# Routing three finished row tiles with one set of VectorE instructions, and a different split of work in the last steps of an attention kernel

## The chip, the cores and the metric

The kernel runs on one core of one Trainium2 chip. The metric is the device time of one execution in microseconds (us); the median of three runs stands for it. TensorE (PE) does the matrix products, VectorE (DVE) and ScalarE (ACT) the elementwise work and the reductions, GpSimd (POOL) some elementwise work and the indirect DMAs, SyncE (SP) issues the other DMAs. Each engine works through its own instructions in their order and waits on semaphores for the others.

## What is computed

Three layers, one behind the other, in float32. First attention over q, k, v of shape (4, 8, 576, 64), in which each row keeps only its 32 largest scores. The result is turned into 2304 rows (tokens) of 512 numbers. Then two mixture-of-experts layers with 8 experts: each row goes to the expert with the largest gate logit. Cut to what matters:

```python
scores = scale * np.matmul(q, k.transpose(0, 1, 3, 2))
kth = np.partition(scores, -32, axis=-1)[..., -32:-31]
scores = np.where(scores >= kth, scores, -1e9)
attn = softmax(scores)                       # exp(x - max) / (sum + 1e-9)
x = np.matmul(attn, v)  ->  rows (2304, 512)
logits = x @ w_gate                          # 8 logits of a row
expert_idx = np.argmax(logits, axis=1)
gate_w = softmax(logits) at expert_idx
out[rows of e] = gate_w * (relu(xe @ w1[e]) @ w2[e])
# second layer: the same on the rows with x @ w_skip > 0, added to x
```

## The kernel before

Attention is cut into 72 groups g = 9 u + j. The unit u is one pair of batches with one pair of heads (8 units: two batch pairs times four head pairs), and j is one of nine row tiles of 128 rows. A group has two halves hh, one for each head, each with a score tile of 128x576.

A loop over steps tau writes out the program. In one step, different stages of different groups stand one behind the other, in an order that the list in `attention` gives: a stage of group g is placed at g plus a fixed distance, and the last six groups have small corrections (`TAIL`). The stages that this document speaks of, with the step of group g in which they stand:

- A1 (g+1): the search for the largest scores on VectorE (14 MAX8 of 82 or 83 columns, then smaller ones). T (g+1): `tm` on POOL.
- Bs (g+4): the signs `sg` on ScalarE, then the products `y` on POOL, two of each. C (g+5): the MAX8 on VectorE that reads `y`.
- Dr, Dm, Dz (g+8): the mask. It is made in one of three ways, by half. "Unmasked first": ScalarE has taken the exponential in the step before (Dx), and VectorE multiplies it by the comparison (`scalar_tensor_tensor`, line 287). Masked first by VectorE (`YS`): a `tensor_scalar` on VectorE (line 266), a subtraction on POOL (line 270), the exponential on ScalarE (line 278). Masked first by ScalarE (`XS`): a Relu on ScalarE (line 269) in place of the `tensor_scalar`. Over six groups, nine of the twelve halves are masked first; in the last `NX` groups none is.
- E (g+9): TensorE turns the probabilities (line 306), and two copies bring them from PSUM to `pT` (ScalarE, line 312; in the last `ND[hh]` groups VectorE, line 310).
- F (g+10): the product with v. FinP, Fin (g+11): the result is turned back, and VectorE writes it, scaled, into the row tile `x` and the shares of the gate logits into `parts` (line 340).
- Ga (g+12), Gr (g+14), for the groups of the units 3 and 7 only, in which a row tile becomes finished: the routing of the row tile. Ga puts seven small VectorE instructions (sum of the shares, maximum, first maximum as a one-hot `gob`) into the list `small`. Gr has an exponential on ScalarE, the ranks on TensorE and then the rest (place in the expert's region, 1/sum, the place as an integer `gix`), again through `small`, at last the indirect DMA (`scatter`, line 576) that writes the 128 rows to their places.

What is in `small` is issued by A1, one instruction behind each of its MAX8s; from step 74 on, with no A1 left, the whole list is issued at the end of each step.

Unit 3 is finished in the middle of attention, unit 7 at its end. The small tiles lg, order and places of a row lie in spare columns of the PSUM tile `s` of the scores. `one_port` (line 70) is a `tensor_scalar` in the form that also writes its accumulator. When all row tiles are scattered, the first expert layer loads its rows.

## Time and profile before

| | |
|---|---|
| median of three runs | 1063.95 us (1061.88 to 1067.97) |
| the profiled execution: time, span | 1056.39 us, 1054.6 us |
| mean granted TensorE clock | 0.954 of full speed |
| busy share of the span | PE 84%, DVE 72%, ACT 64%, POOL 60% |
| attention | from 0 to about 506 us |
| expert layers | from about 508 us to the end |

The shares are means over two parts with different limits. Attention has 20 slices of the 40 of the page: there VectorE is at 90% or more in slice after slice, while in the expert layers TensorE is.

### The profile page before, as it was taken

To read this page: it belongs to the slowest core of one execution; us is meant where nothing else is said; L and a number is where in the kernel's file an instruction comes from. 1 tells how busy PE (TensorE), PEld (TensorE's weight loads), DVE (VectorE), ACT (ScalarE), POOL (GpSimd) and SP (SyncE) were. 2 spreads that over 40 slices of the span, in tenths; PEclk is the share of its full clock that TensorE was granted. 3 is DMA by queue.
4 is the path that set the end of the run, shared out by engine and by line. 5 is a ranking of instruction groups with operands and counts; after the bars stand their busy time and mean duration, and the time that the engine had idled before them with its cause. 6 is when DMAs were issued, how large, how long until landed. Compare 5 with 4: busy or idle time off the path is not lost. (4 is left out here: it accounts for less than half of the span.)

```text
span 1054.6 us, 20835 instructions
## 1 busy us (share of the span) xinstructions
PE 884.0 (84%) x6315; PEld 699.0 (66%) x6315; DVE 759.8 (72%) x3581; ACT 674.5 (64%) x1362; POOL 628.4 (60%) x451
## 2 busy tenths in 40 slices
PE   7477878786777768887699999998998799999994
PEld 5355555554455545555588879877886788899883
DVE  7999999999999999999427545456563356644461
ACT  5599999988898989973335534554553454443340
POOL 2788887887888888863224344344533566564561
PEclk9699999989998999979799999999999899999997
DMA  9992010100302000001635544466633466665520
GB/s 307 320 278 68 2 46 24 46 24 21 109 32 89 22 21 21 2 1 52 225 120 183 171 144 152 140 200 182 188 112 108 149 222 208 217 201 178 167 86 14
DMA packets 55049, 127.88 MB, mean 121 GB/s; under 512 B 8105, under 2 KB 8105, under 8 KB 54864
## 3 DMA queue, kind: packets, MB, share of 16 engines
q1 hardware_dynamic: 48464, 112.89, 34.0%
q0 software_dynamic: 6400, 12.65, 3.2%
q8 instruction: 100, 1.64, 0.6%
q14 instruction: 85, 0.70, 0.2%
HBM read 96.04 MB, written 37.86 MB: 127 GB/s over the span
## 5 line engine op out<-in xcount | busy, mean ns | idle before, releaser
L692 POOL TENSOR_TENSOR w<-raw,w 128x1024 fp32r<-128x1024 f32 x74 | 179.4, 2436 | 192.0 <-ACT w L690 136.8
L224 POOL TENSOR_TENSOR y<-s,sg 128x576 f32<-128x576 f32 x144 | 208.4, 1468 | 52.8 <-ACT sg L221 43.3
L767 PE MATMUL y<-w,h 128*128 128x512 f32 x936 | 228.1, 396 | 8.3 <-DVEq L716 2.2
L743 PE MATMUL hp<-xT,w 128*128 128x192 f32 (+4 forms) x1536 | 213.6, 296 | 5.6 <-DVE h L758 3.0
L743 PEld LDWEIGHTS hp<-xT,w 128*128 128x128 f32 x1536 | 203.7, 190 | 9.8 <-DVE h L758 5.3
L767 PEld LDWEIGHTS y<-w,h 128*128 128x128 f32 x936 | 171.4, 188 | 50.1 <-issue 10.5
L193 DVE MAX8 ca<-s 128x8 f32<-128x82 f32 (+1 forms) x1008 | 160.1, 228 | 5.3 <-ACT s L182 5.3
L270 POOL TENSOR_TENSOR r<-s,r 128x576 f32<-128x576 f32 x96 | 135.7, 1427 | 17.8 <-DVE r L266 15.9
L690 ACT ACTIVATE w<-raw 128x1024 fp32r<-128x1024 f32 x128 | 133.5, 1054 | 0.5 <-ACTq L716 0.5
L758 DVE SCALAR_TENSOR_TENSOR h<-hp,h 128x512 fp32r<-128x512 f32 (+1 forms) x128 | 77.8, 619 | 76.5 <-ACT h L757 76.5
L757 ACT ACTIVATE h<-hp 128x512 fp32r<-128x512 f32 (+1 forms) x128 | 69.8, 545 | 97.0 <-PE hp L743 89.6
L306 PE MATMUL m<-ident,p 128*128 128x128 f32 x576 | 97.7, 297 | 37.9 <-DVE parts L340 19.2
L306 PEld LDWEIGHTS m<-ident,p 128*128 128x128 f32 x576 | 65.3, 147 | 79.9 <-ACT p L278 25.0
L221 ACT ACTIVATE sg<-s,tm 128x576 f32<-128x576 f32 x144 | 112.1, 800 | 8.4 <-POOL tm L212 8.4
L692 DVE TENSOR_TENSOR w<-raw,w 128x1024 fp32r<-128x1024 f32 x54 | 96.0, 1777 | 21.5 <-ACTq L716 12.8
L97 PE MATMUL s<-kT,qT 64*128 64x288 f32 x512 | 83.3, 444 | 24.2 <-ACT gex L596 14.6
L231 DVE MAX8 my<-y 128x8 f32<-128x576 f32 x144 | 101.6, 745 | 0.7 <-POOL y L224 0.6
L182 ACT ACTIVATE s<-s 128x1152 f32<-128x1152 f32 (+1 forms) x73 | 81.8, 1122 | 22.1 <-PE s L97 18.2
L134 PE MATMUL m<-pT,v 128*64 128x128 f32 (+1 forms) x1280 | 88.3, 285 | 7.2 <-ACT pT L312 5.4
L134 PEld LDWEIGHTS m<-pT,v 128*64 128x64 f32 x1280 | 69.8, 148 | 20.3 <-ACT pT L312 9.4
L312 ACT ACTIVATE pT<-m 128x512 f32<-128x512 f32 x137 | 76.9, 612 | 6.8 <-PE m L306 6.8
L278 ACT ACTIVATE p<-r,neg 128x576 f32<-128x576 f32 x96 | 75.4, 790 | 8.2 <-POOL r L270 7.9
(136 smaller groups left out, 1254.4 us busy)
## 6 DMA issues: line engine op xcount, KB each, us to landing
raw<-in_moe_w_dram SPq DMA_DIRECT2D x128, 512.0 KB, 4.4
x<-zrow SPq DMA_DIRECT2D x16, 1028.0 KB, 17.9
xg<-x SPq DMA_DIRECT2D x56, 257.0 KB, 3.7
v<-in_v_dram SPq DMA_DIRECT2D x8, 576.0 KB, 3.8
kT<-in_k_dram SPq DMA_DIRECT2D x7, 576.0 KB, 4.3
qT<-in_q_dram SPq DMA_DIRECT2D x7, 576.0 KB, 5.7
out_dram<-yo,ix POOLq DMA_INDIRECT x40, 4.9
kT<-in_k_dram SPq DMA_DIRECT2D x2, 288.0 KB, 3.5
```

Source lines behind the costliest of these rows:

```text
L97: nc.tensor.matmul(p[:, c, :288], d["qT"][h, b, t * 128:t * 128 + 128], d["kT"][h, b, cs], start=True, stop=True)
L134: nc.tensor.matmul(po[i * 64:i * 64 + 64, cs], d["vt"][:, b, i, c] if c < 4 else d["v8"][i * 64:i * 64 + 64, b], pts[i][:, c, cs] if c < 4 ...
L193: nc.vector.max(out=ca[:, c], in_=e["s"][hh][:, cut[c]:cut[c + 1]])
L221: nc.scalar.activation(sg, e["s"][hh], AF.Sign, bias=bt["tm"][:, w:w + 1], scale=-ONE_BELOW, accum_out=bt["ac"][:, w:w + 1])
L224: nc.gpsimd.tensor_mul(y, e["s"][hh], sg)
L231: nc.vector.max(out=bt["my"][:, 2 * i + hh, 8:], in_=e["y"][hh])
L270: nc.gpsimd.tensor_tensor(r, e["s"][hh], r, op=OP.subtract)
L306: nc.tensor.transpose(pp[:, c], e["p"][:, hh, c * 128:c * 128 + 128], ident)
L690: nc.scalar.activation(t[:, 0], raw, AF.Copy)
L692: eng.tensor_tensor(t[:, 1], raw, t[:, 0].bitcast(F32), op=OP.subtract)
L743: nc.tensor.matmul(p[:, :W], self.w1(g, c)[:, a, fs], x[:, c, b, :W], start=(i == 0), stop=(i == 11))
L767: nc.tensor.matmul(p, self.HT[f][:, a, js], self.W2[f // 2][:, b, f % 2 * 512:f % 2 * 512 + 512], start=(f + a + b == 0), stop=(f == 7 and ...
```

## The change

Three row tiles that lie side by side (j = 0 to 2, 3 to 5, 6 to 8) share one tile `x` and one tile `parts`, and are routed together when the third is finished; the very last one (j = 8 of the last unit) is routed alone, and the two before it as a pair. The instructions of the routing work on 128x3x8 elements, with `tensor_tensor` and `tensor_reduce` in place of the forms that take one scalar per row. Besides, `NX` goes from 8 to 3 (the groups 64 to 68 keep the mixed masks), and `ND` from (0, 7) to (0, 0) (ScalarE makes all copies to `pT`).

```diff
-NX = 8
-ND = (0, 7)
+NX = 3
+ND = (0, 0)
...
-            x[bp, j] = ev.xp.tile([128, HP * 128 + 2], F32, name="x", bufs=11)
+            x[bp, j // 3] = ev.xp.tile([128, 3, HP * 128 + 2], F32, name="x", bufs=4)
...
+        n = {NG - 2: 2, NG - 1: 1}.get(g, 3 if j % 3 == 2 else 0)
+        return (bp, j // 3, j % 3 + 1 - n, n) if hp == HP - 1 and n else None
...
+def gate_tiles(tc, ev, sb, x, parts, rt, places):
...
+    def rest():
+        nc.scalar.activation(ed, ed, AF.Exp)
+        nc.gpsimd.tensor_copy(x[:, :, Dm + 1], ev.tok[:, rt:rt + n])
+        p = ev.ps.tile([128, 4, 8], F32, name="m", bufs=ev.mb)
+        nc.tensor.matmul(p[:, :n + 1], ev.tri, ob[:, :n + 1], start=True, stop=False)
+        for k in range(n, 0, -1):
+            nc.tensor.matmul(p[:, n + 1 - k:n + 1], ev.ones, ob[:, :k], start=False, stop=(k == 1))
...
+    def empty():
+        nc.gpsimd.memset(ob[:, n], 0.0)
+        v.tensor_reduce(out=lg, in_=parts.rearrange("p t h e -> p t e h"), op=OP.add, axis=AX.X)
...
+    return [empty,
+            lambda: v.tensor_reduce(out=f[:, :, 0], in_=lg, op=OP.max, axis=AX.X),
+            lambda: v.tensor_tensor(order, lg, wide(f[:, :, 0:1]), op=OP.is_ge),
+            lambda: v.tensor_tensor(ed, lg, wide(f[:, :, 0:1]), op=OP.subtract),
+            lambda: v.tensor_tensor(order, order, ev.rev8[:, None, :].to_broadcast([128, n, 8]), op=OP.mult),
+            lambda: v.tensor_reduce(out=f[:, :, 1], in_=order, op=OP.max, axis=AX.X),
+            lambda: v.tensor_tensor(ob[:, :n], order, wide(f[:, :, 1:2]), op=OP.is_equal)], rest, [
+            lambda: v.tensor_tensor(row, at[0][:, :n], base[:, None, :].to_broadcast([128, n, 8]), op=OP.add),
+            lambda: v.tensor_tensor(base, at[0][:, n], base, op=OP.add),
+            lambda: v.tensor_tensor(mine, row, ob[:, :n], op=OP.mult),
+            lambda: v.tensor_reduce(out=f[:, :, 3], in_=ed, op=OP.add, axis=AX.X),
+            lambda: v.tensor_reduce(out=f[:, :, 2], in_=mine, op=OP.add, axis=AX.X),
+            lambda: v.tensor_scalar(f[:, :, 3], f[:, :, 3], 1e-9, None, op0=OP.add),
+            lambda: v.tensor_copy(ix[:, :n], f[:, :, 2]),
+            lambda: v.reciprocal(x[:, :, Dm], f[:, :, 3])] + [
+            lambda t=t: scatter(tc, ev, ev.rows[0], ix[:, t:t + 1], x[:, t], ev.group) for t in range(n)]
```

In the changed program two of these carry line numbers that are named later: the `tensor_scalar` that adds 1e-9 is line 642 and the cast to `tix` line 643; both read and write SBUF.

VectorE, middle of attention (unit 3). Before, the second half of one row tile's routing stands between the MAX8s of A1; `gf`, `gob` and `gix` are its small tiles:

```order
L564 TENSOR_TENSOR s<-m,base_90 128x8
L565 TENSOR_TENSOR base_90<-m,base_90 128x8
L193 MAX ca<-s 128x8
L601 TENSOR_SCALAR gf<-gf 128x1
L193 MAX ca<-s 128x8
L568 SCALAR_TENSOR_TENSOR gf<-s,gob 128x8
L193 MAX ca<-s 128x8
L602 RECIPROCAL x<-gf 128x1
L193 MAX ca<-s 128x8
L603 CAST gix<-gf 128x1
```

In the changed program the second half for three row tiles, with `tf`, `ted`, `tob` and `tix` in their place, ends like this:

```order
L639 TENSOR_TENSOR s<-s,tob 128x24
L193 MAX ca<-s 128x8
L640 TENSOR_REDUCE tf<-ted 128x3
L193 MAX ca<-s 128x8
L641 TENSOR_REDUCE tf<-s 128x3
L193 MAX ca<-s 128x8
L642 TENSOR_SCALAR tf<-tf 128x3
L193 MAX ca<-s 128x8
L643 CAST tix<-tf 128x3
L193 MAX ca<-s 128x8
L644 RECIPROCAL x<-tf 128x3
```

One such set stands in every third step in place of one in each, and the addition and the cast work on three elements of a partition instead of one.

POOL, from the last `tm` (step 72) to the end of attention. Before, the products `y` of the groups 69 to 71 stand alone, and then come nine copies and nine scatters in turn:

```order
L212 TENSOR_SCALAR tm<-my 128x6
L224 TENSOR_TENSOR y<-s,sg 128x576 x6
L597 COPY x<-tok 128x1
L576 DMA x_82<-x,gix 18432x514
L597 COPY x<-tok 128x1
L576 DMA x_82<-x,gix 18432x514
```

In the changed program the subtractions `r` of the groups 65 to 68 stand between them, and the scatters come three, three, two and one at a time:

```order
L212 TENSOR_SCALAR tm<-my 128x6
L270 TENSOR_TENSOR r<-s,r 128x576 x2
L224 TENSOR_TENSOR y<-s,sg 128x576 x2
L270 TENSOR_TENSOR r<-s,r 128x576 x2
L224 TENSOR_TENSOR y<-s,sg 128x576 x2
L270 TENSOR_TENSOR r<-s,r 128x576 x2
L224 TENSOR_TENSOR y<-s,sg 128x576 x2
L270 TENSOR_TENSOR r<-s,r 128x576
L627 MEMSET tob 128x8
L619 COPY x<-tok 128x3
L573 DMA x_82<-x,tix 18432x514 x3
```

Seven more POOL instructions of 576 columns stand behind the last `tm` than before, and an eighth in front of it.

## Rows read from the trace of the kernel before

**Rows 1.** Busy time by stretch: stretch, length, engines (count), TensorE clock, DMA share, GB/s

```profile
250.00:300.00 50.00, 34.91 (x321) 23.25 (x320) 49.55 (x332) 42.99 (x106) 40.61 (x39) 0.97 0.22 74
460.00:480.00 20.00, 15.89 (x128) 10.45 (x124) 19.59 (x63) 13.29 (x33) 10.68 (x7) 0.91 0.00 0
```

**Rows 2.** Timeline, VectorE: A1 with one row tile's routing, A1 without (start, us)

```profile
252.02 0.24 DVE L193 MAX8 ca<-s 128x8 f32<-128x83 f32 x1
...
255.27 0.30 DVE L201 MAX8 m<-ca 128x8 f32<-128x21 f32 x2
...
310.31 2.10 DVE L193 MAX8 ca<-s 128x8 f32<-128x83 f32 x14
312.32 0.30 DVE L201 MAX8 m<-ca 128x8 f32<-128x21 f32 x2
```

**Rows 3.** By line: VectorE instructions, count: shortest/median/longest ns, first and last start

```profile
L266 DVE TENSOR_SCALAR r<-s,kths x13: 508/511/733, 105.9 to 215.3; 128x576 f32<-128x576 f32 x13
L266 DVE TENSOR_SCALAR r<-s,kths x15: 508/661/2670, 308.3 to 438.3; 128x576 f32<-128x576 f32 x15
L601 DVE TENSOR_SCALAR gf<-gf x9: 133/133/135, 245.9 to 304.6; 128x1 f32<-128x1 f32 x9
L568 DVE SCALAR_TENSOR_TENSOR fx<-fx,ob x22: 154/156/1907, 560.0 to 817.5; 128x8 f32<-128x8 f32 x22
L287 DVE SCALAR_TENSOR_TENSOR p<-s,kths,e x17: 792/811/1953, 446.7 to 488.2; 128x576 f32<-128x576 f32 x17
```

**Rows 4.** Timeline, POOL and VectorE: products beside A1, and in the last steps

```profile
252.79 2.77 POOL L224 TENSOR_TENSOR y<-s,sg 128x576 f32<-128x576 f32 x2 [1.32 <-ACT sg L221]
...
457.55 0.24 POOL L212 TENSOR_SCALAR tm<-my 128x6 f32<-128x6 f32 x1 [0.88 <-DVE my L201]
459.83 3.29 POOL L224 TENSOR_TENSOR y<-s,sg 128x576 f32<-128x576 f32 x2 [2.04 <-ACT sg L221]
...
459.94 1.92 DVE L287 SCALAR_TENSOR_TENSOR p<-s,kths,e 128x576 f32<-128x576 f32 x1
...
469.09 3.72 POOL L224 TENSOR_TENSOR y<-s,sg 128x576 f32<-128x576 f32 x2 [1.17 <-ACT sg L221]
```

**Rows 5.** Timeline, VectorE in the last steps: both halves of one row tile's routing

```profile
472.36 0.26 DVE L513 TENSOR_REDUCE s<-parts 128x8 f32<-128x64 f32 x1
...
473.52 0.76 DVE L231 MAX8 my<-y 128x8 f32<-128x576 f32 x1
...
482.73 0.17 DVE L564 TENSOR_TENSOR s<-m,base 128x8 f32<-128x8 f32 x1
...
483.35 0.81 DVE L287 SCALAR_TENSOR_TENSOR p<-s,kths,e 128x576 f32<-128x576 f32 x1
```

**Rows 6.** Groups of instructions, 308 to 444 us, ScalarE: count, busy us, mean ns

```profile
L278 ACT ACTIVATE p<-r,neg 128x576 f32<-128x576 f32 x32 | 25.2, 793 | 3.4 <-POOL r L270 3.3
L312 ACT ACTIVATE pT<-m 128x512 f32<-128x512 f32 x42 | 23.5, 616 | 3.1 <-PE m L306 3.1
L269 ACT ACTIVATE r<-s,kb 128x576 f32<-128x576 f32 x17 | 13.4, 790 | 0.0
```

**Rows 7.** Timeline, TensorE: the turns of the groups 68, 70 and 71

```profile
476.91 0.66 PE L306 MATMUL m<-ident,p 128*128 128x128 f32 x4 [0.23 <-ACT oT L323]
...
486.45 0.66 PE L306 MATMUL m<-ident,p 128*128 128x128 f32 x4 [0.24 <-ACT oT L323]
...
490.65 0.66 PE L306 MATMUL m<-ident,p 128*128 128x128 f32 x4 [0.30 <-ACT oT L323]
```

**Rows 8.** Timeline, the end: last row tile on VectorE, POOL's last scatters

```profile
499.35 0.29 DVE L340 TENSOR_TENSOR x<-m,ri 128x128 f32<-128x128 f32 x1 [0.47 <-PE m L328]
...
504.16 0.98 POOL L576 DMA_INDIRECT x<-x,gix  x1 [0.72 <-DVE gf L601]
...
505.62 0.98 POOL L576 DMA_INDIRECT x<-x,gix  x1 [0.28 <-POOL x L597]
```

**Rows 9.** Who waited for whom, SyncE's queue, 480 to 520 us: total, times, longest

```profile
SPq L699 <- DMA x<-x,gix: 9.3, 1, 9.3
```

More of the change, by code (lines that the diff above doesn't have):

```diff
@@ L113, in spare_places @@
     ev.onehot = [s[:, 0, 1, 288 + 54 * i:342 + 54 * i].rearrange("p (a b) -> p a b", b=9) for i in range(2)]
-    ev.logits = [s[:, 1, 0, 288 + 8 * i:296 + 8 * i] for i in range(4)]
-    ev.placed = [s[:, 1, 1, 288 + 8 * i:296 + 8 * i] for i in range(4)]
+    ev.gates = [[s[:, 1, h, 288 + 48 * i + 24 * w:312 + 48 * i + 24 * w].rearrange("p (t e) -> p t e", e=8)
+                 for h in range(2) for w in range(2)] for i in range(2)]
     tc.nc.vector.tensor_copy(ev.counts, ev.iosel[:, None, :].to_broadcast([128, 6, 9]))
@@ L334, in Fin @@
         bp, hp = divmod(u, HP)
-        if hp == 0:
-            x[bp, j] = ev.xp.tile([128, HP * 128 + 2], F32, name="x", bufs=11)
-            parts[bp, j] = ev.xp.tile([128, HP * 2, 8], F32, name="parts", bufs=11)
-        for out, at, w in ((x[bp, j][:, hp * 128:hp * 128 + 128].rearrange("p (a b) -> p a b", a=2), 0, 64),
-                           (parts[bp, j][:, hp * 2:hp * 2 + 2], 128, 8)):
+        if hp == 0 and j % 3 == 0:
+            x[bp, j // 3] = ev.xp.tile([128, 3, HP * 128 + 2], F32, name="x", bufs=4)
+            parts[bp, j // 3] = ev.xp.tile([128, 3, HP * 2, 8], F32, name="parts", bufs=4)
+        rows, shares = x[bp, j // 3][:, j % 3], parts[bp, j // 3][:, j % 3]
+        for out, at, w in ((rows[:, hp * 128:hp * 128 + 128].rearrange("p (a b) -> p a b", a=2), 0, 64),
+                           (shares[:, hp * 2:hp * 2 + 2], 128, 8)):
             nc.vector.tensor_tensor(out, e["po"][:, at:at + 2 * w].rearrange("p (a b) -> p a b", a=2),
@@ L342, in Fin, with gated @@
         del G[g]
-    def row_tile(g):
+    def gated(g):
         u, j = divmod(g, 9)
         bp, hp = divmod(u, HP)
-        return (bp, j) if hp == HP - 1 else None
+        n = {NG - 2: 2, NG - 1: 1}.get(g, 3 if j % 3 == 2 else 0)
+        return (bp, j // 3, j % 3 + 1 - n, n) if hp == HP - 1 and n else None
     def Ga(g):
-        at = row_tile(g)
+        at = gated(g)
         if at:
-            rt = at[0] * 9 + at[1]
-            lg = ev.logits[rt % 4]
-            a, rest, c = gate_rows(tc, ev, sb, x[at], rt, lg, ev.placed[rt % 4])
-            small.append(lambda: head_logits(tc, parts[at], lg))
+            bp, k, t, n = at
+            a, rest, c = gate_tiles(tc, ev, sb, x[bp, k][:, t:t + n], parts[bp, k][:, t:t + n], bp * 9 + k * 3 + t,
+                                    ev.gates[(k + (n == 1)) % 2])
             small.extend(a)
@@ L508, in turn_and_gate @@
         nc.vector.tensor_copy(ev.turn[h, :, 128 + a * 8:136 + a * 8], ev.wg1[h])
-def head_logits(tc, parts, lg):
-    tc.nc.vector.tensor_reduce(out=lg, in_=parts.rearrange("p h w -> p w h"), op=OP.add, axis=AX.X)
 def gate_logits(tc, ev, sb, x, lg):
@@ L604, in gate_rows @@
         lambda: scatter(tc, ev, ev.rows[0], ix[:, 0:1], x, ev.group)]
+def gate_tiles(tc, ev, sb, x, parts, rt, places):
+    nc = tc.nc
+    v, n = nc.vector, x.shape[1]
+    Dm = x.shape[2] - 2
+    lg, order, row, mine = [p[:, :n] for p in places]
+    f = sb.tile([128, 3, 8], F32, name="tf", bufs=2)[:, :n]
+    ed = sb.tile([128, 3, 8], F32, name="ted", bufs=2)[:, :n]
+    ob = sb.tile([128, 4, 8], BF, name="tob", bufs=2)
+    ix = sb.tile([128, 3], I32, name="tix", bufs=2)
+    wide = lambda t: t.to_broadcast([128, n, 8])
+    base, at = ev.base[0], []
+    def rest():
[5 more added lines that the diff above has]
+            nc.tensor.matmul(p[:, n + 1 - k:n + 1], ev.ones, ob[:, :k], start=False, stop=(k == 1))
+        at.append(p)
+    def empty():
[17 more added lines that the diff above has]
+            lambda t=t: scatter(tc, ev, ev.rows[0], ix[:, t:t + 1], x[:, t], ev.group) for t in range(n)]
```

2 lines of the change are left out of this document (1 added, 1 removed).

## The prediction

> **What bounds the kernel now.** First the busy time by stretch. From 250 to 300 us, where unit 3 is routed, VectorE works 49.55 of 50 us, ScalarE 43.0 and POOL 40.6; from 460 to 480 us, near the end of attention, it is 19.59, 13.29 and 10.68 of 20 [rows 1]. So in both places VectorE sets the pace, and its time counts in full until another engine takes over. Then the end: SyncE's first load of the expert layer stands waiting 9.3 us, until the last scatter has landed [rows 9], and that scatter starts at 505.62 [rows 8]. What ends attention is thus the chain from the last row tile over the scatters on POOL. All that comes later is the same in both programs, so I count to the start of the last scatter.
>
> **Routing in the middle (unit 3).** An A1 whose fourteen MAX8s carry one whole set of small instructions takes from 252.02 to 255.27, 3.25 us; one without takes 310.31 to 312.32, 2.01 [rows 2]. The difference, 1.24 us, is the price of one row tile: twelve instructions at 0.103 each, far less than the 0.13 to 0.26 us that each lasts, since they overlap. Nine row tiles cost 11.2. The new set has fifteen on VectorE (7 and 8), 1.55 at that price. It is also wider: the first sum reads 192 elements instead of 64, and some ten others 24 instead of 8, together about 290 elements. A MAX8 of 576 columns lasts 0.76 us [rows 5] and one of 83 lasts 0.24 [rows 2], 1.05 ns per element, so 0.3 us. That is 1.85 a set and 5.6 for three sets: **5.6 us saved** (6.5 if the width costs nothing, 4.5 if twice that). No other engine stands in the way there: ScalarE and POOL have 7 and 9 us free in 50 [rows 1].
>
> **Two of the fifteen may wait for POOL.** Some VectorE instructions stop while POOL works. The `tensor_scalar` of line 266, SBUF to SBUF, takes 0.51 us at best and up to 2.67; the one with two SBUF inputs (line 287) 0.81 and up to 1.95 [rows 3]. One of these, from 459.94 for 1.92 us, lies beside a pair of products that began at 459.83, and that pair took 3.29 us instead of 2.77 [rows 4]: they take turns. Size doesn't protect: an instruction of eight elements with two SBUF inputs (line 568 in the expert layer) has a median of 0.156 us and a longest of 1.907 [rows 3]. The new set keeps most of its operands in PSUM, but the addition (line 642) and the cast (line 643) go from SBUF to SBUF. Their forerunners did so too, on one element, and never took more than 0.135 us (line 601) [rows 3]. So the trace bounds the wait from both sides. Nothing, if three elements behave as one. Up to 2.67 - 0.51 = 2.16 for each of six instructions, 13 us, if they behave as line 266. Where in A1 they stand decides the size. At 0.144 + 0.103 us per MAX8 with its companion, the addition comes some 1.4 us into A1. The pair of products starts 0.77 after an A1 [rows 2, 4] and each lasts 1.39: the addition waits 0.8 for the first, the cast, 0.25 later, 1.2 for the second, 2.0 in all; where the pair starts with A1 it is 1.3. I take 1.8 a set, **5.4 us lost**. I take this end since these are the kinds of operation that line 266 is, on several elements, and a single element is the exception among the rows.
>
> [...]
>
> **The end (groups 64 to 71).** Off VectorE go eight multiplications of line 287 (0.81 to 1.95 us each [rows 3]) and seven copies, and four sets instead of nine for unit 7. Chained, one row tile there costs 1.16 + 0.62 = 1.78 us [rows 5], 16 in all; the four new sets, some 2.3 each by the same rows, 9. Onto it come four `tensor_scalar`s of 0.51. That is some 18 us less, but not what attention gains, since other engines get the work. ScalarE: seven copies of 0.62 and four Relus of 0.79 (the exponentials only change their kind) [rows 6]; from 460 to 480 us that takes it from 13.3 to at most 19 of 20. POOL: eight subtractions of 1.39. Behind the last `tm` (457.8 at its end [rows 4]; 0.7 earlier, as a multiplication is gone before it) it must do seven subtractions and six products, 13 x 1.39 = 18.1 us, in an order that lets nothing pass. Three of the new `tensor_scalar`s fall into that row and hold it 0.5 each (3.29 - 2.77), 1.5. So the last subtraction, of group 68, ends at 457.1 + 18.1 + 1.5 = 476.7, and its exponential (0.79, and 0.3 to get through) at 477.8. Before, TensorE began to turn group 68 at 476.91 [rows 7]: **0.9 later**. Everything that VectorE saves up to there is hidden behind POOL.
>
> From group 68 to 71 TensorE then took 13.74 us, 4.58 a group (the last 4.20, with 0.3 of waiting) [rows 7], held up by copies on VectorE. Its own work is about 3.9 a group, 11.7: **2.0 earlier**. From the turn of group 71 (490.65) to the last row tile (499.35 + 0.28) it was 9.0; I estimate 1.1 less: 0.6 for the last copy, which then stands on ScalarE, and 0.5 for two exponentials of the routing that no longer stand there. From there to the last scatter it was 6.0 [rows 8]: now the pair has two scatters where one was, and one more in the line is 0.98 plus a gap of 0.28, **1.3 later**. The cast of the last set also waits until the scatters of the second set have landed, two sets before, which I expect 1 us before it matters. Together 0.9 - 2.0 - 1.1 + 1.3 = **0.9 us saved**, uncertain by 3 either way.
>
> **Sum.** -5.6 + 5.4 - 0.9 = -1.1 us. The profiled execution took 1056.39 and would take 1055.3; it is 0.7% faster than the median of the runs, 1063.95, so on the median I put the same difference: **1062.8 us**. From no change a measurement can tell about 0.5% here, 5.3 us.
>
> **Rivals.** A, three elements wait no more than one: only the 5.4 falls away, -6.5, **1057.4**. For it speaks line 601; against it line 266. B, POOL is no brake at the end: its 20 us of idle time between products [rows 4] might take the subtractions in, and groups come at TensorE's 3.9 from `tm` to the turn of group 68, four of them 15.6 in place of 20.2: 4.6 better, **1058.2**, with A 1052.8. Against it: POOL's order is fixed, and each `y` waits for a `sg` that stands behind copies. C, the slower one: POOL and ScalarE go in lockstep at steps 73 to 75. Each subtraction pair (2.8) must pass through an exponential (0.8), TensorE's turn (ten matmuls at 0.66 for four, with gaps some 1.9 [rows 7]), two copies (1.2) and two signs (1.6, of the Relu's shape) before the next products; if none of it overlaps, a step takes 8.3 instead of the 4.63 of before (459.83 to 469.09 in two steps [rows 4]), three steps 11 us. With 0.9 no longer counted that gives -1.1 - 0.9 + 11 = +9, **1073**. It decides for slower once each step is 2.4 us longer than in my row of thirteen. Against it: in the middle of attention the same mix runs at 90% or more of VectorE's time, so the overlap works there, with nine buffers of `s`.
>
> **How the numbers follow.** My forecast 0.45, A 0.30, B with or without A 0.15, C 0.10. Faster by over 0.5% (below 1058.6): 0.68 of A, 0.75 of B, 0.1 of the forecast, 0.36. Slower: 0.7 of C and a little of the forecast, 0.08. The rest, 0.56, within 0.5%. The range leaves out most of C above and the lower part of B below: 1054.5 to 1067. The forecast alone reaches from 1059.5 to 1066, by the 3 us at the end and by 1.3 to 2.0 a set.
>
> **What would show it.** Lines 642 and 643, in the middle of attention, should last 0.8 to 1.4 us instead of 0.13, each up to the end of a product; if they last 0.14, A holds. An A1 with the second half should grow by 0.9 without them. The turn of group 68, counted from the last `tm`, should start at +20, and POOL should be without a gap between; a gap at each `y` means C, an earlier turn B. The groups 68 to 71 should come 3.9 us apart, and the last scatter should start some 15 us after the turn of group 71. The prediction is wrong if line 266 or 287 elsewhere meets POOL more or less often than before: of the fifteen of line 266 from 308 to 444 us some cost 2 us more [rows 3], and the phase of the engines may shift.

## The result: slower by 0.8%

The changed kernel takes 1068.93 us (median of 13 runs, 1065.67 to 1073.35); the kernel before, beside it, 1061.33 (13 runs, 1056.02 to 1067.97). The ratio is 1.0079, with an interval of 1.0055 to 1.0102. The forecast, 1062.8 with a range up to 1067, was wrong.

The profiled executions differ by 10.2 us (1056.39 and 1066.61). The starts of A1 (its first MAX8) and of the scatters cut them into stretches:

| stretch | before | after | difference |
|---|---|---|---|
| start to A1 of step 39 (nothing routed yet) | 229.24 | 229.97 | +0.7 |
| A1 of step 39 to A1 of step 52 (unit 3 routed) | 95.08 | 100.40 | **+5.3** |
| A1 of step 52 to A1 of step 72 | 129.65 | 130.08 | +0.4 |
| A1 of step 72 to the last scatter | 51.65 | 52.29 | **+0.6** |
| last scatter to the end | 548.99 | 552.01 | **+3.0** |

These differences are not equally firm. The stretch of unit 3 is: 99.8 to 100.4 us in the five traces with the scatters, masks and waits of the changed kernel (after, e1, e3, e7, e8), 94.6 to 95.2 in the five that route it as before, without a burst (before, e2, e12, e15, e16). The end of the changed kernel takes 50.1 to 52.3 us in the traces whose edits leave it alone, and the time from the last scatter to the end lies between 548.8 and 561.0 us over the 20 traces. So the +0.6 and the whole of the +3.0 can't be told from the difference between two executions; of the +3.0, the loss in the first expert can (below).

The busy times of the two stretches shown in [rows 1], in the same columns (PE, PEld, DVE, ACT, POOL, then clock, DMA share, GB/s), are now:

```profile
250.00:300.00 50.00, 33.95 (x283) 23.27 (x282) 49.80 (x248) 36.20 (x83) 36.22 (x33) 0.85 0.19 68
460.00:480.00 20.00, 13.76 (x105) 9.85 (x106) 13.17 (x57) 15.98 (x40) 17.20 (x13) 0.83 0.01 1
```

From 250 to 300 us VectorE is still busy all the time, but with 248 instructions instead of 332, and the other engines do less: the time has gone into instructions that stand. At the end VectorE has become free (13.17 instead of 19.59) and POOL is the busy one (17.20 instead of 10.68), as forecast.

**Where VectorE stands in the middle.** The timeline of VectorE in the first routed set shows lines 642 and 643 (the forecast was 0.8 to 1.4 us each instead of 0.13 to 0.15):

```profile
257.74 0.99 DVE L642 TENSOR_SCALAR tf<-tf 128x3 f32<-128x3 f32 x1
258.64 0.23 DVE L193 MAX8 ca<-s 128x8 f32<-128x82 f32 x1
258.80 1.30 DVE L643 CAST tix<-tf 128x3 int32<-128x3 f32 x1
```

In the other two sets they take 0.84 and 0.14, 0.88 and 1.30. Over 0.15 for each, that is 4.6 us in all. Larger is what was not forecast. The timelines of VectorE and POOL behind the second set's scatters:

```profile
286.89 6.77 DVE L287 SCALAR_TENSOR_TENSOR p<-s,kths,e 128x576 f32<-128x576 f32 x1
...
283.88 1.06 POOL L573 DMA_INDIRECT x<-x,tix  x1 [1.25 <-DVE x L644]
285.24 0.98 POOL L573 DMA_INDIRECT x<-x,tix  x1 [0.30 <-issue]
286.52 0.98 POOL L573 DMA_INDIRECT x<-x,tix  x1 [0.30 <-issue]
287.50 1.44 POOL L270 TENSOR_TENSOR r<-s,r 128x576 f32<-128x576 f32 x1
288.86 2.79 POOL L224 TENSOR_TENSOR y<-s,sg 128x576 f32<-128x576 f32 x2
291.56 0.13 POOL L627 MEMSET tob<- 128x8 bf16 x1
291.62 1.42 POOL L270 TENSOR_TENSOR r<-s,r 128x576 f32<-128x576 f32 x1
```

The three scatters hold POOL from 283.88 to 287.50, and then four products follow without a gap. One instruction of VectorE, 0.81 us of work, stands through all four until 293.66. In [rows 4] such an instruction got in behind the first product, and the next product took 1.9 us instead of 1.4; here each product takes its 1.4, so VectorE never had its turn. The longest of line 266 from 260 to 330 us is 3.47 us (before: 2.27). Summed over all of lines 266 and 287 between steps 39 and 52, the time above 0.51 and 0.81 us is 11.9 us instead of 4.7. So the middle reads +5.3 = 4.6 (lines 642 and 643) + 7.2 (lines 266 and 287) - 6.5. The last is a remainder; the A1s show most of it as the saving of the shorter routing. Those of steps 39 to 51 take 11.15 us more before than thirteen bare ones of 2.01 us, and 9.64 in the changed kernel, of which 4.6 are the two waits: 5.0 without them, 6.1 saved.

**The end.** POOL works without a gap from the last `tm` on, where [rows 4] had products alone. Timeline of POOL, and the turn of group 68 on TensorE:

```profile
464.03 0.24 POOL L212 TENSOR_SCALAR tm<-my 128x6 f32<-128x6 f32 x1 [2.24 <-DVE my L201]
464.83 2.77 POOL L270 TENSOR_TENSOR r<-s,r 128x576 f32<-128x576 f32 x2 [0.56 <-DVE r L266]
467.56 3.00 POOL L224 TENSOR_TENSOR y<-s,sg 128x576 f32<-128x576 f32 x2
...
481.89 1.40 POOL L270 TENSOR_TENSOR r<-s,r 128x576 f32<-128x576 f32 x1
...
484.24 0.55 PE L306 MATMUL m<-ident,p 128*128 128x128 f32 x3
```

The turn comes 20.2 us behind `tm` (forecast +20; before 19.4). The groups 68 to 71 then follow in 10.2 us (484.24 to 494.43; forecast 11.7; 13.74 in [rows 7]). From there it goes worse than forecast. The rows of TensorE and POOL around 499 us:

```profile
499.01 0.18 PE L621 MATMUL m<-tob,tri 128*128 128x32 bf16 x1 [1.18 <-POOL tob L627]
...
497.86 0.97 POOL L573 DMA_INDIRECT x<-x,tix  x1 [0.30 <-issue]
498.83 0.13 POOL L627 MEMSET tob<- 128x8 bf16 x1
...
504.51 0.29 DVE L341 TENSOR_TENSOR x<-m,ri 128x128 f32<-128x128 f32 x1 [1.00 <-PE m L328]
...
512.73 0.99 POOL L573 DMA_INDIRECT x<-x,tix  x1 [0.28 <-POOL x L619]
```

The memset of `tob`, 0.1 us of work, stands behind the three scatters of the first set, the ranks on TensorE wait for it, and what follows on TensorE waits behind them. From the turn of group 71 to the last row tile it takes 10.4 us (forecast 7.9), from there to the last scatter 7.9 (504.80 to 512.73; forecast 7.3; answers to [rows 8]). The wait for the memset is 1.18 us of this; what the rest is shows under e7 and e8.

**The expert layers**, which the forecast took as equal, lose 2.5 us in the first expert: from its first turned rows to those of the second it takes 49.36 us instead of 46.82; all later experts agree within 0.7. The nine kernels with sets in unit 3 and 26 transposes all take 49.0 to 49.6 us there. The windows of before, then of after, count from the idle transposes (`keep_busy`) on:

```profile
508.00:514.00 6.00, 5.80 (x27) 5.43 (x27) 2.20 (x8) 2.19 (x4) 0.00 (x0) 0.50 0.40 103
514.00:520.00 6.00, 3.34 (x19) 2.32 (x20) 2.67 (x4) 2.28 (x4) 0.00 (x0) 0.99 0.98 354
```
```profile
514.00:518.00 4.00, 3.96 (x20) 3.99 (x21) 2.20 (x8) 0.00 (x0) 0.00 (x0) 0.54 0.21 70
518.00:522.00 4.00, 1.75 (x13) 1.53 (x12) 0.00 (x0) 2.19 (x4) 0.00 (x0) 0.89 0.74 202
522.00:526.00 4.00, 2.97 (x13) 2.20 (x11) 1.55 (x3) 1.79 (x3) 0.00 (x0) 0.50 0.98 323
526.00:530.00 4.00, 3.28 (x8) 2.75 (x9) 1.22 (x2) 0.60 (x1) 0.00 (x0) 0.50 1.02 416
```

Before, the 26 idle transposes ended 0.2 us ahead of the rows' arrival, and the granted clock was 0.99 from 514 to 520 us. After, they ended 2.2 us ahead of it; TensorE stood idle, and the granted clock was back at 0.50 from about 521 to 531 us.

### The profile page after: what moved, and what is told of

Its sections match the earlier page's. It is cut to its first block, busy times and chain, and to the rows that moved or that the text cites. A ratio compares the mean times of both kernels' runs of the same rounds, so it can differ in the third digit from the quotient of the medians.

```text
span 1064.7 us, 20657 instructions
## 1 busy us (share of the span) xinstructions
PE 895.0 (84%) x6304; PEld 709.7 (67%) x6304; DVE 752.2 (71%) x3415; ACT 676.8 (64%) x1352; POOL 635.4 (60%) x455
## 5 line engine op out<-in xcount | busy, mean ns | idle before, releaser
L224 POOL TENSOR_TENSOR y<-s,sg 128x576 f32<-128x576 f32 x144 | 205.6, 1450 | 52.5 <-ACT sg L221 46.6
L784 PEld LDWEIGHTS hp<-xT,w 128*128 128x128 f32 x1536 | 205.3, 191 | 10.2 <-DVE h L799 5.9
L193 DVE MAX8 ca<-s 128x8 f32<-128x82 f32 (+1 forms) x1008 | 156.4, 227 | 5.4 <-ACT s L182 5.4
L270 POOL TENSOR_TENSOR r<-s,r 128x576 f32<-128x576 f32 x104 | 148.1, 1438 | 16.9 <-DVE r L266 13.6
L221 ACT ACTIVATE sg<-s,tm 128x576 f32<-128x576 f32 x144 | 112.0, 799 | 10.1 <-POOL tm L212 10.1
L733 DVE TENSOR_TENSOR w<-raw,w 128x1024 fp32r<-128x1024 f32 x54 | 96.0, 1778 | 20.6 <-ACTq L757 11.9
L97 PE MATMUL s<-kT,qT 64*128 64x288 f32 x512 | 88.8, 468 | 23.6 <-DVE tob L636 12.0
L134 PE MATMUL m<-pT,v 128*64 128x128 f32 (+1 forms) x1280 | 92.0, 293 | 6.8 <-ACT pT L312 6.6
L278 ACT ACTIVATE p<-r,neg 128x576 f32<-128x576 f32 x104 | 81.5, 787 | 17.0 <-POOL r L270 14.8
L134 PEld LDWEIGHTS m<-pT,v 128*64 128x64 f32 x1280 | 72.8, 153 | 20.5 <-ACT pT L312 11.1
L312 ACT ACTIVATE pT<-m 128x512 f32<-128x512 f32 x144 | 80.3, 608 | 4.9 <-PE m L306 4.7
```

Of the source, the lines that this page charges most:

```text
L97: nc.tensor.matmul(p[:, c, :288], d["qT"][h, b, t * 128:t * 128 + 128], d["kT"][h, b, cs], start=True, stop=True)
L134: nc.tensor.matmul(po[i * 64:i * 64 + 64, cs], d["vt"][:, b, i, c] if c < 4 else d["v8"][i * 64:i * 64 + 64, b], pts[i][:, c, cs] if c < 4 ...
L193: nc.vector.max(out=ca[:, c], in_=e["s"][hh][:, cut[c]:cut[c + 1]])
L221: nc.scalar.activation(sg, e["s"][hh], AF.Sign, bias=bt["tm"][:, w:w + 1], scale=-ONE_BELOW, accum_out=bt["ac"][:, w:w + 1])
L224: nc.gpsimd.tensor_mul(y, e["s"][hh], sg)
L270: nc.gpsimd.tensor_tensor(r, e["s"][hh], r, op=OP.subtract)
```

## The experiments

The ratio is to the kernel before on the same chip, and the last three columns are read from the profiled execution of each (us; "first expert" is the distance named above). That execution can lie some us off the median: 1053.60 of e10, whose median is 1061.18, or 1057.80 of e17, whose median is 1051.57.

| run | ratio [95% interval] | step 39 to 52 | step 72 to last scatter | first expert |
|---|---|---|---|---|
| before | 1 | 95.1 | 51.7 | 46.8 |
| after | 1.0079 [1.0055, 1.0102] | 100.4 | 52.3 | 49.4 |
| e1 sets alone | 1.0053 [1.0034, 1.0073] | 99.8 | 50.4 | 49.6 |
| e2 split alone | 0.9971 [0.9944, 0.9999] | 94.6 | 50.1 | 46.7 |
| e3 40 transposes | 1.0048 [1.0028, 1.0068] | 100.0 | 51.0 | 46.8 |
| e4 single port | 1.0012 [0.9986, 1.0038] | 97.3 | 52.5 | 49.0 |
| e5 spread | 1.0049 [1.0030, 1.0068] | 101.4 | 50.1 | 49.3 |
| e6 burst, before | 1.0020 [1.0001, 1.0039] | 96.9 | 51.5 | 46.7 |
| e7 memset on VectorE | 1.0032 [1.0018, 1.0047] | 100.1 | 49.6 | 49.3 |
| e8 pair ahead | 1.0039 [1.0023, 1.0056] | 100.3 | 49.7 | 49.6 |
| e9 four edits | 1.0047 [1.0018, 1.0076] | 98.3 | 49.7 | 46.0 |
| e10 four and spread | 1.0010 [0.9980, 1.0040] | 94.0 | 49.4 | 47.7 |
| e11 relief | 1.0110 [1.0075, 1.0146] | 107.0 | 52.3 | 49.0 |
| e12 sets at the end | 0.9987 [0.9963, 1.0010] | 94.7 | 51.0 | 49.5 |
| e13 stand-ins | 1.0101 [1.0070, 1.0132] | 92.2 | 51.5 | 49.3 |
| e14 bursts moved | 1.0068 [1.0043, 1.0093] | 91.8 | 52.1 | 49.1 |
| e15 extra scatters, before | 1.0128 [1.0101, 1.0155] | 94.7 | 51.4 | 49.6 |
| e16 split, ahead | 0.9975 [0.9951, 0.9999] | 95.2 | 50.0 | 48.2 |
| e17 bursts in the gap | 0.9925 [0.9897, 0.9952] | 89.5 | 50.4 | 49.5 |
| e18 the same, first set spread | 0.9922 [0.9892, 0.9953] | 87.9 | 48.9 | 46.9 |

**Which half of the change costs (e1, e2).** e1 is the changed kernel with the old split, e2 the kernel before with the new one:

```diff
-NX, ND = 3, (0, 0)        # e1
+NX, ND = 8, (0, 7)
-NX, ND = 8, (0, 7)        # e2
+NX, ND = 3, (0, 0)
```

> Routing in sets of three alone; the end of attention keeps the first kernel's split (NX = 8, ND = (0, 7)). Theory (the sets cost in the middle of attention): the stretch from A1 of step 39 to A1 of step 51 stays near 93 us (88.2 before), and the time stands 4 to 8 us above the kernel before, 1065 to 1069. Rival (the split of the last groups is what costs): within 3 us of the kernel before, 1058 to 1064, and 88 to 89 us in that stretch.

> The new split of the last groups alone (NX = 3, ND = (0, 0)); routing one row tile at a time as before. Theory (the sets cost in the middle): 88 us in the stretch of steps 39 to 51, and the time within 3 us of the kernel before, since POOL's row of thirteen takes back what VectorE saves. Rival (the split costs): 4 to 8 us above the kernel before. Third case, the split is a gain that the sets hide: 4 us or more below it.

The expectations count to step 51, where e1 takes 92.9 us and e2 87.6; the table goes on to step 52. The sets cost, 4.7 us in the middle. The split gains a little: e2 is as fast as before in the middle and 1.6 us faster at the end, and in all 0.3% faster, with an interval that ends just below 1. The rival for e1 falls.

**The first expert (e3).**

```diff
-IDLE = (26, 44)
+IDLE = (40, 44)
```

> The changed kernel with 40 instead of 26 idle transposes ahead of the first expert (IDLE = (40, 44)), so that TensorE does not stand idle before the rows land. Theory (the 3 us lost in the expert layers come from a clock that falls to 0.5 in that gap): granted clock 1.0 from the first turned rows on, instead of 0.5 until 531 us, and 2 to 3 us less than the changed kernel, 1066. Rival (chance, or another cause): the same 1069 as the changed kernel, or more, since the transposes delay the rows.

The first expert is back at 46.8 us, with the granted clock at 1.00 from 518 us on, and the ratio falls by 0.3%. So the loss in the first expert goes with the granted clock: 49.4 us where it was 0.50 behind 2.2 idle us, 46.8 where it stayed at 1.00. What that is worth in all, this trace does not show: from the last scatter to the end it takes 555.2 us, 3.2 more than that of the changed kernel, since the sixth expert and a later one lose 3.0 and 2.1 us; and the intervals of the two ratios overlap. The remedy is not sure either: of six kernels with 40 transposes two (e12, e17) still took 49.5; there TensorE was busy 0.1 and 0.4 of 2 us (from 514 and 510 us on), and the granted clock was 0.50 from 518 to 524 and from 514 to 520 us.

**The two small instructions (e4).**

```diff
-            lambda: v.tensor_scalar(f[:, :, 3], f[:, :, 3], 1e-9, None, op0=OP.add),
-            lambda: v.tensor_copy(ix[:, :n], f[:, :, 2]),
+            lambda: one_port(tc, ev, f[:, :, 3], f[:, :, 3], 1e-9, OP.add),
+            lambda: one_port(tc, ev, ix[:, :n], f[:, :, 2], 0.0, OP.add),
```

> The changed kernel with lines 642 and 643 written as a tensor_scalar with an accumulated output, the form of line 72, that never took more than 0.2 us in attention. Theory (their waits for POOL's products cost, 0.7 to 1.2 us each in five of the six): both at 0.15 us in all sets, and 2.5 to 5 us less than the changed kernel, 1064 to 1066.5. Rival (the bursts of three scatters cost, and what these two lines give back is lost at line 287 or 266, which meet POOL's next work): within 1.5 us of the changed kernel, with line 287 or 266 at 3 us and more after each burst.

The lines of the two in this run, from VectorE's groups between 255 and 313 us (x3: the three sets):

```profile
L72 DVE TENSOR_SCALAR_CACHE_REDUCE tf<-tf x3: 141/147/147, 257.2 to 305.7; 128x3 f32<-128x3 f32 x3
L72 DVE TENSOR_SCALAR_CACHE_REDUCE tix<-tf x3: 140/146/149, 257.4 to 305.9; 128x3 int32<-128x3 f32 x3
```

Neither waits any more, and the stretch of unit 3 is 3.1 us shorter, less than the 4.6 us of waits: lines 266 and 287 stand 0.4 us more in it (the longest three 3.51, 6.75 and 3.46 us), and where the other 1.1 us went is not shown. Both theories of the expectation held in part. The ratio fell by 0.67%, more than these 3 us; three of its twelve runs lie at 1055.65 to 1058.75 and the others above 1063, the profiled one at 1067.40, so the trace does not show what the three did.

**Scatters apart, scatters together (e5, e6).** In e5 the scatters of a set stand one per A1; in e6 the kernel before issues three in a row:

```diff
+    gap = [lambda: None] * (12 if rt < 9 else 0)                  # e5
...
-            lambda t=t: scatter(...) for t in range(n)]
+            step for t in range(n) for step in [lambda t=t: scatter(...)] + gap * (t < n - 1)]
...
+            held.append(c[-1])                                    # e6, in Gr
+            small.extend(c[:-1])
+            if at[1] % 3 == 2 or at[0]:
+                small.extend(held)
+                del held[:]
```

> The changed kernel with the three scatters of a set in unit 3 set apart, one for each A1 (twelve empty places between two of them in the row of small instructions), as they lay before. Theory (three scatters in a row, 3.6 us on POOL, put POOL behind, so that lines 266 and 287 then meet products without a gap and stand 2.9, 6.8 and 3.5 us): no such instruction over 2.7 us between 250 and 325 us, the stretch from A1 of step 39 to A1 of step 51 at 88 to 90 us instead of 93.4, and 4 to 6 us less than the changed kernel, 1063 to 1065. Rival (the long stalls come from the phase of the engines, not from the burst): within 1.5 us of the changed kernel, with a stall of 5 us or more somewhere in that stretch.

> The kernel before, routing one row tile at a time, with nothing changed but that the scatters of unit 3 are issued three in a row, behind the third set of each three. Theory (the burst alone makes the stalls): line 266 or 287 at 3 us or more behind at least one burst, the stretch of steps 39 to 51 at 90.5 to 93 us instead of 88.1, and 2.5 to 5 us above the kernel before. Rival (the burst is harmless where the sets are narrow): within 1.5 us of the kernel before.

e5 refutes the burst as I had stated it. To step 51 it takes 89.5 us, as expected, but then a stall of 4.51 us comes at 326.47, behind the last of the spread scatters (324.95), and to step 52 the stretch is no shorter. The ratio is 0.3% lower, but the two intervals overlap, and what the trace has less, 2.2 us, lies at the end, which the edit leaves alone. e6 costs 1.8 us in the stretch (90.0 us to step 51) and 0.2% in all, with stalls of 3.16 and 3.46 us behind two bursts: a cost, but less than expected.

**The end (e7, e8).**

```diff
-        nc.gpsimd.memset(ob[:, n], 0.0)          # e7
+        v.memset(ob[:, n], 0.0)
...
+        while g == NG - 1 and small:             # e8, ahead of Fin's multiplications
+            small.pop(0)()
```

> The changed kernel with the memset of line 627 on VectorE instead of POOL, where it stood behind three scatters and held TensorE's ranks for 1.2 us at 499 us. Theory: the ranks of the second set of unit 7 start right after the products of group 70, the last row tile is finished 1.2 to 2 us earlier against the turn of group 71 (8.1 to 8.9 us instead of 10.1), and the time is 1 to 2 us less than the changed kernel, 1067. Rival (TensorE then waits for the ones of line 636, or the slower clock eats it): no change, 1069.

> The changed kernel with the small instructions that are waiting put ahead of the last row tile's multiplications, so that the first half of the pair (groups 69 and 70) lies before the last row tile instead of behind it. Theory: from the last row tile to the start of the last scatter 6.3 to 6.7 us instead of 8.2, and 1.5 us less than the changed kernel, 1067.4. Rival (the first half then holds the last row tile up, or the pair's scatters become the last thing to wait for): no change, 1069.

e7: from the turn of group 71 to the start of the last row tile 7.6 us (492.63 to 500.21) instead of 10.1. e8: from the last row tile to the last scatter 7.0 instead of 8.2. Both traces have the last scatter 2.6 us nearer to the last A1.

For e8, 1.2 us of this are its edit: from the end of the row tile to the last scatter the nine traces with sets at the end and without that edit take 7.80 to 7.95 us, e8 6.70. For e7, the 2.5 us are not all the memset's. In e5, whose end is that of the changed kernel, TensorE waits as long for the same memset, and yet the row tile starts 7.9 us behind the turn of group 71. What differs is the granted clock. The ranks of e5, and then the 2 us that begin 6 us behind the turn of group 71, of the changed kernel and of e5 (the clock stands third from the end):

```profile
499.21 0.18 PE L622 MATMUL m<-tob,tri 128*128 128x32 bf16 x1 [1.17 <-POOL tob L628]
```
```profile
500.43:502.43 2.00, 2.00 (x35) 1.76 (x36) 1.27 (x10) 0.00 (x0) 0.00 (x0) 0.55 0.03 8
```
```profile
500.64:502.64 2.00, 1.54 (x25) 1.10 (x23) 0.76 (x7) 0.28 (x1) 0.71 (x1) 1.00 0.01 4
```

In the changed kernel ScalarE's copy of `oT` for group 70 came at 499.60, behind the ranks (499.01), TensorE waited 0.68 us more for it, and then its granted clock fell to 0.55; in e5 the copy came at 498.14, ahead of the ranks (499.21), and the clock stayed at 1.00. Why the copy came late is not shown. Against e5 the memset is worth 0.3 us of that step (7.6 instead of 7.9), and with the memset on VectorE the step can still be slow: e12 takes 10.5.

The ratios fell by 0.47% and 0.40%, more than the end explains; another 1.6 us of what their traces show lie between steps 52 and 72, where nothing was edited, and are not explained.

**All together (e9, e10, e12).** e9 has the edits of e3, e4, e7 and e8, e10 also that of e5. e12 has those of e9, but routes unit 3 one row tile at a time:

```diff
+        n = 1 if bp == 0 else {NG - 2: 2, NG - 1: 1}.get(g, 3 if j % 3 == 2 else 0)
...
+            if bp == 0:
+                a, rest, c = gate_rows(tc, ev, sb, x[bp, k][:, t], k * 3 + t, lg, ev.placed[g % 4])
```

> The changed kernel with four of the single edits together: lines 642 and 643 in the form of line 72, the memset on VectorE, the waiting instructions ahead of the last row tile, 40 idle transposes. If they add up as timed alone (the ratios to the kernel before fell by 0.0067, 0.0047, 0.0040 and 0.0031, of which the last three meet in the same few us at the end, so I count half of each), 1.0079 - 0.0067 - 0.006 = 0.995, 1056. Rival (they are shifts of phase and not costs removed): no better than the best of them alone, 1.001, 1062. The long stall of line 287 behind the second burst should still be there (6.7 us).

> The same four edits and the scatters of unit 3 set apart. Theory (the burst is a cost of its own): 2 to 4 us less than the run without it, no stall over 3 us up to 325 us. Rival (the spread scatters only move the long stall to a later step, as to 326.5 us when they were spread alone): within 1.5 us of that run.

> Unit 3 routed one row tile at a time as before, unit 7 in sets, with the new split of the last groups, the memset on VectorE, the waiting instructions ahead of the last row tile and 40 idle transposes. Theory (the sets cost in the middle and gain at the end): 88 us from step 39 to 51, last A1 to last scatter at 49 us, and 4 to 7 us less than the kernel before, 1054 to 1057. Rival (the sets cost at the end too): not faster than the new split alone, 1058.

The single gains did not add up: e9 is no better than e3 alone, with line 287 at 6.71 us in its trace. e10 is better, 94.0 in the stretch, but again with a stall of 4.52 us behind a spread scatter. e12 is not faster than the split alone (0.9987 against 0.9971): the sets gained nothing at the end, where POOL sets the pace.

**Less work on POOL (e11).**

```diff
-        return (g % 6, hh) in XS + YS and g < NG - NX
+        return (g % 6, hh) in XS + YS and g < NG - NX and g not in (35, 36, 38, 39, 41, 42)
```

> The changed kernel with less for POOL in the steps in and behind the three bursts: the masks of groups 35, 36, 38, 39, 41 and 42 all in the form of line 287, so that POOL has ten subtractions of 1.39 us less, ScalarE five Relus less, and VectorE five times 0.81 and five times 0.3 us more, 5.6 us. Theory (rows of POOL's work without a gap make the long stalls): no stall over 2.7 us between 260 and 325 us, which gives back 7 us there, so 1 to 2 us less than the changed kernel, 1067. Rival (the long stalls don't come from POOL's rows): they stay and the stretch from step 39 to 51 grows by 5 us, 1074.

This went against the theory and as the rival had it. With ten products less on POOL, line 287 stands 4.96, 5.47 and 5.42 us, and each of the three begins 0.3 to 0.8 us behind the issue of the third scatter of a burst. The number of products is not what decides. I therefore went through every meeting in the fourteen traces so far: an instruction of line 266 or 287 that has waited for 0.1 us or more when one of POOL's products ends and the next begins within 0.25 us. Either the next product runs first at its 1.4 us (turn lost), or VectorE gets in (turn won). Every instruction that lost a turn had begun within 6.1 us of the issue of a scatter.

**Scatter or backlog (e13, e14, e15).** e13 takes the second and third burst of unit 3 out, issues these six scatters one per step at steps 63 to 68, and puts work of the same length without a transfer in their place; e14 has no such stand-ins. (What is held back needs more buffers, five of `x` and four of `tix`; so in e17 and e18.) e15 is the kernel before with thirteen more scatters:

```diff
+            if at[0] == 0 and at[1]:                       # e13 and e14, in Gr
+                held.extend(c[-3:])
+                c = c[:-3] + [lambda t=t: stand_in(tc, ev, x[at[0], at[1]][:, t]) for t in range(3)]   # e14: c[:-3]
...
+        if g == 50:
+            for late in held:
+                small.extend([late] + [lambda: None] * 13)
...
+def stand_in(tc, ev, x):                                   # e13
+    tc.nc.gpsimd.tensor_copy(ev.idle, x[:, 512:514])
+    for i in range(2):
+        tc.nc.gpsimd.memset(ev.zrow[:, :512], 0.0)
...
+        if 41 <= g < 54:                                   # e15, in Gr
+            small.append(lambda: scatter(tc, ev, ev.rows[1], ev.zix[:, g - 41:g - 40], ev.zrow))
```

> The changed kernel with the second and third burst of unit 3 taken out (their six scatters are issued one per step at steps 63 to 68) and work without any transfer put in their place on POOL: for each scatter a copy of two columns and two memsets of 512 columns, about as long as a scatter. Theory S (an instruction of VectorE loses its turn to POOL's products only while rows of a scatter are under way, some 6 us from its issue): behind the stand-ins every turn is won, lines 266 and 287 at 2.7 us at most between 275 and 330 us, and 4 to 6 us less in the stretch to step 52 than the changed kernel (100.4). Rival B (POOL's backlog alone makes the stall, with or without a transfer): line 287 at 6 us or more behind the second place again.

> The same without the stand-ins: the second and third burst of unit 3 are only moved to steps 63 to 68, one scatter per step. Both theories expect no stall over 2.7 us from 275 to 330 us; what VectorE's small instructions save shows there undisturbed: 92 to 95 us to step 52 instead of 100.4 (95.1 before). At steps 63 to 70 theory S expects lost turns, stalls of 2 to 4.5 us that the changed kernel does not have there, rival B none.

> The kernel before with thirteen additional scatters, one in each A1 of steps 54 to 66, which write rows of zeros over zeros; nothing else is changed. Before, all turns of lines 266 and 287 in steps 52 to 72 were won (stalls of 1.6 to 2.0 us, one of 2.67 that waited for a single product). Theory S: among the meetings with rows of products within 6 us of a scatter at least one turn in two is lost, stalls of 2.9 to 5 us, and the time grows by more than the 13 issues are worth to POOL, 3 to 10 us. Rival B: the scatters shift the phase, turns are won as before, at most 2.7 us, and the time stays within 3 us.

In e13 the stand-ins hold POOL 3.8 us at either place, and four and six products follow with nothing but a memset between; still no instruction of lines 266 and 287 takes over 1.83 us there. The timelines of VectorE and POOL at the third place:

```profile
312.08 1.68 DVE L266 TENSOR_SCALAR r<-s,kths 128x576 f32<-128x576 f32 x1
...
306.87 1.10 POOL L658 MEMSET zrow<- 128x512 f32 x2
307.94 2.77 POOL L270 TENSOR_TENSOR r<-s,r 128x576 f32<-128x576 f32 x2
310.67 2.77 POOL L224 TENSOR_TENSOR y<-s,sg 128x576 f32<-128x576 f32 x2
313.39 3.01 POOL L270 TENSOR_TENSOR r<-s,r 128x576 f32<-128x576 f32 x2
```

The instruction waits for one product, and the next pair takes 3.01 us instead of 2.77, since VectorE had its turn. It is the only meeting behind the stand-ins of e13, but not the only one against the backlog: in the end of the changed kernel, where POOL works 18.47 of the 18.50 us from 464.80 to 483.30, all three meetings are won, with the last scatter over 150 us before. In e15, steps 52 to 72, which had won every turn, lose four. VectorE and POOL, without any set:

```profile
363.52 4.50 DVE L287 SCALAR_TENSOR_TENSOR p<-s,kths,e 128x576 f32<-128x576 f32 x1
...
362.00 1.04 POOL L578 DMA_INDIRECT x<-zrow,zix  x1 [0.16 <-issue]
363.08 0.26 POOL L212 TENSOR_SCALAR tm<-my 128x6 f32<-128x6 f32 x1
363.29 1.41 POOL L270 TENSOR_TENSOR r<-s,r 128x576 f32<-128x576 f32 x1
364.65 2.75 POOL L224 TENSOR_TENSOR y<-s,sg 128x576 f32<-128x576 f32 x2
```

From step 52 to 72 it takes 142.5 us instead of 129.6, 12.9 more for thirteen scatters, over the 3 to 10 expected. The time of lines 266 and 287 above 0.51 and 0.81 us grows by as much there, from 8.0 to 21.1 us, so it is these instructions and not the issues themselves. e14 and e13 lose the same way where their six late scatters went (140.3 and 141.2, with stalls of 5.57, 5.42 and two of 4.5 us), which is why they are slower in all although unit 3 takes 91.8 and 92.2 us instead of 100.4. Of theory S it holds that a scatter ahead makes VectorE lose its turns, and the backlog alone falls as a cause. That the rows of the scatter have to be under way does not hold. The third scatter of the second burst was issued at 286.52; the busy times of the changed kernel behind it (DMA share and GB/s stand last):

```profile
286.50:289.00 2.50, 1.66 (x22) 1.10 (x21) 2.50 (x4) 1.80 (x7) 2.48 (x3) 1.00 0.54 211
289.00:293.60 4.60, 0.00 (x0) 0.00 (x0) 4.60 (x3) 2.33 (x5) 4.04 (x4) 0.87 0.00 0
```

From 289 us on no DMA moves anything, and still the products that began at 290.2 and 291.6 went ahead of line 287.

**A version that beats both (e16 to e18).** e16 is e2 with the edit of e8. e17 is e9 with the second and third burst of unit 3 held back until POOL's last product is through; e18 spreads the first set's scatters too:

```diff
+        while g == 68 and held:                  # e17 and e18, at the head of E
+            held.pop(0)()
...
+    gap = [lambda: None] * (11 if rt == 0 else 0)       # e18
```

> The new split of the last groups alone (the best so far), and the small instructions that wait put ahead of the last row tile's multiplications. There only a few of them stand behind it, so 0 to 0.7 us less than the split alone, 1057.5 to 1058.2; if the row tile is held up by them, as much more.

> The run with the four edits (single-port form of lines 642 and 643, memset on VectorE, waiting instructions ahead of the last row tile, 40 idle transposes), and the second and third burst of unit 3 held back until POOL's last product of attention is through, into the 11 us in which POOL stood idle there (six scatters, 7.7 us). Theory S: turns are won all through steps 46 to 72, 87 to 89 us from step 39 to 52 instead of 95.1 in the kernel before and 100.4 in the changed one, last A1 to last scatter 49 to 50 us; 6 to 9 us less than the kernel before, 1052 to 1055. Rival (the six scatters at the end hold up those of unit 7, or cost elsewhere): no better than the split alone, 1058.

> The same, with the three scatters of the first set of unit 3 set apart, one per A1. Theory S: the stall of 2.9 us behind the first burst goes, 1 to 2.5 us less than the run with the burst kept. Rival (a lost turn comes back at another of the three steps): the same within 1 us, or up to 2 us more.

e16 is e2 again. e17 is 0.75% faster than before (1051.57 against 1060.36 us), e18 0.78% (1052.14). The nine executions of e17 fall into two groups, five up to 1051.57 and four from 1055.51 on, and the profiled one belongs to the second, so its trace shows the stretch of unit 3 but not the median. e18 has no stall over 2.6 us left there, and the stretch is 1.6 us shorter, but in all it is as fast as e17, as the rival had it. In e17 POOL issues the six where it would stand idle:

```profile
471.58 1.42 POOL L270 TENSOR_TENSOR r<-s,r 128x576 f32<-128x576 f32 x1
473.14 1.41 POOL L580 DMA_INDIRECT x<-x,tix  x1
...
480.45 0.97 POOL L580 DMA_INDIRECT x<-x,tix  x1 [0.30 <-issue]
481.41 0.22 POOL L626 COPY x<-tok 128x3 f32<-128x3 f32 x1
486.50 0.98 POOL L580 DMA_INDIRECT x<-x,tix  x1 [4.87 <-issue]
```

Line 287 between 260 and 330 us, of the changed kernel and of e17 (min/median/max in ns):

```profile
L287 DVE SCALAR_TENSOR_TENSOR p<-s,kths,e x4: 802/812/6773, 279.2 to 329.0; 128x576 f32<-128x576 f32 x4
```
```profile
L287 DVE SCALAR_TENSOR_TENSOR p<-s,kths,e x5: 800/811/2050, 277.2 to 323.5; 128x576 f32<-128x576 f32 x5
```

## Why the prediction was wrong, by its steps

- **Routing in the middle, 5.6 us saved: right.** The A1s show 6.1: 11.15 us over bare ones before (forecast 11.2), 5.04 in e4, where nothing in them waits (forecast 5.6). (The twelve instructions of the sum are right: Ga issues six in the kernel before, not seven; and 4.5 us for twice the width should be 4.7.) That e17 takes 5.6 us less than before in all of steps 39 to 52 (89.5 against 95.1) meets the forecast by luck, since six of the nine scatters are gone from there.
- **Lines 642 and 643, 5.4 us lost: right in kind and nearly in size**, 4.6 us in the trace. The five that waited, 0.84 to 1.30 us long, each ended within 0.05 us of the end of one of POOL's products, and in the form with an accumulated output the two took 0.14 to 0.15 us in all three sets (e4). Rival A falls.
- **The sum is the step that failed.** It priced the routing's own instructions and took lines 266 and 287 to stand as often as before; behind "No other engine stands in the way there" it counted POOL's 9 free us in 50. What the scatters do to VectorE had no term: 7.2 us in unit 3. The kernel before has as many scatters there and lost one turn; what has changed is which products of POOL stand behind each. The burst alone cost 1.8 us there (e6), so how many turns are lost depends on where the scatters fall. The prediction had named this as what would make it wrong, without a price. It also read "they take turns" from one row of a stretch without scatters, and took 2.67 us as the longest wait.
- **The end, 0.9 us saved: 0.6 lost, within what one execution differs from another.** The turn of group 68 at +20 was right, and with it POOL as the bound (rivals B and C fall). The groups 68 to 71 came 1.5 us faster than forecast. The step from the turn of group 71 to the last row tile was wrong by 2.5 us in this trace and by 0.3 in that of e5: the memset on POOL behind three scatters, 1.2 us, was not counted among the waits, and the granted clock of 0.55, where it came, not at all. e7 without the memset took 7.9 us to the end of that tile, as forecast.
- **"All that comes later is the same in both programs": wrong by 3 us in these traces.** The program is the same, but 26 idle transposes no longer reached to the rows' arrival; 2.5 us of it, in the first expert, come again in every such kernel.
- 5.3 + 0.4 + 0.6 + 3.0 and 0.7 that was there before any routing make, unrounded, the 10.1 us between the two spans.

## What to carry to other kernels

An instruction moved on one engine is priced by its own row, but what it starts on another engine must be priced too: here the turns that VectorE lost behind DMAs on POOL cost more (7.2 us) than the shorter routing saved (6.1). Six of POOL's nine indirect DMAs of unit 3, moved to where POOL had no products behind them, took the stretch from 98.3 us (e9) to 89.5 (e17); where VectorE and POOL share work as here, that is the place to try. And a block that only keeps TensorE busy until data arrive has to be set again whenever the data's arrival moves: here it ended 2.2 us too early, and the first expert lost 2.5 us at a granted clock of 0.50.

## What the runs showed of the hardware that was not expected

In the 20 traces of this study, 48 instructions of line 287 (two SBUF inputs) and line 266 (a `tensor_scalar` from SBUF to SBUF) met two of POOL's products in a row and had begun within 6.1 us of the issue of an indirect DMA on POOL. 45 of them did not get in between the products and lost at least one turn; none of the 336 others that met two products in a row did. (Many of the 45 are the same place in kernels that differ little. No meeting lies between 6.1 and 9.7 us, so the limit may be anywhere there. The three that won are in e10 and e18.) One that has lost then stood until the row of products had a gap, up to 6.77 us for 0.81 us of work, where the 336 stood 2.05 us at most.

The waits lasted through up to four products of 1.4 us. VectorE was already waiting each time when the product that went ahead of it began: in the stall of 6.77 us since 286.89, and the four began at 287.50, 288.86, 290.2 and 291.62. It is not the rows under way, which had ended 2.7 us before the last of these four, and not the length of the work on POOL, since 3.8 us of work without a transfer did not do it: behind it no instruction of the two lines took over 1.83 us (e13). Why the issue of a scatter does it, and for how long, is not shown. Whether a scatter whose rows go nowhere would do it wasn't tried.
